# Routing tokens to sorted rows batch by batch, with each expert's weights fetched once

## The chip, the cores and the metric

The kernel runs on one core of a Trainium2 chip. The metric is device time in microseconds (us). A core has a matrix engine (TensorE, PE in the profile; its weight loads are PEld), a vector engine (VectorE, DVE), a scalar engine (ScalarE, ACT), a general one (GpSimd, POOL), a queue engine that issues transfers (SyncE, SP), and 16 DMA engines. SBUF is the memory on the chip, with 128 partitions; PSUM takes the results of TensorE in eight banks.

## The reference

Two blocks follow each other. The first is a gated linear recurrence over 768 steps for 4 batches and 8 heads of width 48; the second routes each of the 3072 tokens to one of 8 experts and scales the expert's output by the token's gate.

```python
# attention: batch 4, heads 8, seq 768, head_dim 48
scale = np.minimum(mag, 0.999) / (mag + 1e-06)      # mag = |a_re + i a_im|
for t in range(S):
    S_re, S_im = ar*S_re - ai*S_im + k_t (x) v_t, ar*S_im + ai*S_re
    y[:, :, t] = q_t . S_re
x = y.transpose(0, 2, 1, 3).reshape(3072, 384)
# experts: E = 8, D = 384, F = 1024
logits = x @ w_gate
expert_idx = np.argmax(logits, axis=1)
gate_w = softmax(logits)[arange, expert_idx]
for e in range(E):
    xe = x[expert_idx == e]
    out[expert_idx == e] = gate_w[..., None] * (np.maximum(xe @ w1[e], 0.0) @ w2[e])
```

With this input the experts get 354, 406, 392, 388, 370, 421, 338 and 403 tokens. Everything is float32.

## The kernel before

Attention is written as a list of operations with estimated durations, which a small list scheduler puts in order for each engine. Per batch: gates are loaded and limited, VectorE scans them (`front`), corrects (`fix`) and folds them into q and k (`fold`), packs go by DMA to head tiles (KX, QX), and TensorE does the chunked attention. At the end of a chunk of 128 tokens (last group of heads), the rows are transposed, multiplied with the gate's weights, and stored:

```python
if g == G - 1:
    rows = state["row", b, c]
    px = pe(6, across, rows, ...)            # 3 transposes of xf
    turned_x = act(DM, lambda: A.copy(xt, px_ps), [px], ...)
    lg = pe(3, logits, [turned_x], ...)      # lg_ps[:, c, :] = x @ wgate
    away = dma(5.0, lambda ...: Q.dma_start(x_hbm[r0:r0 + 128, 0:DM]..., xf[:, c, :]), rows)
...
copy = act(C * E, lambda: A.copy(lg_all[:, b * C:(b + 1) * C, :], lg_ps), [lg], first=1)
```

After attention comes a general path for gates that the fast scan cannot take: two loops whose count of trips, 0 here, is loaded into a register of every engine.

```python
n_blk = nc.values_load(trips[0:1, 0:1], min_val=0, max_val=S // BL, ...)
n_til = nc.values_load(trips[0:1, 1:2], min_val=0, max_val=NT, ...)
with tc.For_i(0, n_blk, 1) as i0:
    ...   # [cut: the recurrence step by step]
with tc.For_i(0, n_til, 1) as ti:
    ...   # [cut: logits of its rows]
```

Then all tokens are routed at once. Each expert's tokens fill whole tiles of 128 places, 31 tiles in all (`NTILE = NT + E - 1`), and two index tables are made: `idx`, the token at each place, and `widx`, the weight rows of each tile.

```python
tt(sub, lg_all, bc(red(lg_all, "mx", ALU.max)[:, :, None], full), ALU.subtract)
...   # [cut: softmax, one-hot, ranks by two matmuls, prefix sums, slots]
for t in range(NT):
    nc.tensor.matmul(ids, lhsT=A[:, t, :], rhs=V[:, t]..., start=(t == 0), stop=(t == NT - 1))
```

The expert part runs tile by tile. It gathers the rows and that tile's weights (3.1 MB) with indirect transfers:

```python
for j in range(NTILE):
    gather(xs, x_hbm[:, :], idx[:, j:j + 1])
    gather(w1t, w1[:, :], widx[:, j:j + 1])
    gather(w2t, w2[:, :], widx[:, j:j + 1])
    for d in range(DT):                                   # 3 transposes
        nc.tensor.transpose(xt_ps[:, d, :], xs[:, d * 128:d * 128 + 128], ident)
    nc.vector.tensor_copy(xt, xt_ps)
    for f in range(FT):                                   # 8 x 3 products, 128 columns
        for d in range(DT):
            nc.tensor.matmul(h_ps[:, f, :], lhsT=w1t[:, c:c + 128], rhs=xt[:, d, :], ...)
    nc.scalar.activation(ht[:, 0:FT // 2, :], h_ps[:, 0:FT // 2, :], func=ACT.Relu)
    nc.vector.tensor_scalar_max(ht[:, FT // 2:, :], h_ps[:, FT // 2:, :], 0.0)
    for f in range(FT):                                   # 8 products, 384 columns
        nc.tensor.matmul(o_ps, lhsT=ht[:, f, :], rhs=w2t[:, f * DM:f * DM + DM], ...)
    nc.vector.tensor_scalar_mul(y, o_ps, xs[:, DM:W])     # gate
    nc.gpsimd.indirect_dma_start(out=out[:, :], out_offset=...idx[:, j:j + 1]..., in_=y, ...)
```

Of the kernel before, what the change touches and what calls it, by code (L numbers as in the profile page):

```python
# [9 lines left out]
FP32 = mybir.dt.float32  # L10
# [23 lines left out]
W = DM + 1  # L34
LEAST = 1e-20
# [100 lines left out]
def gateloop_then_moe(ctx, tc, q, k, a_re, a_im, v, wg, w1, w2, out):  # L136
    nc = tc.nc
    x_hbm = nc.dram_tensor("x_hbm", (N + 1, W), FP32, kind="Internal").ap()

# [20 lines left out]
    with tc.tile_pool(name="zero", bufs=1) as setup:  # L160
        zrow = setup.tile([1, W], FP32, name="zrow")
        nc.vector.memset(zrow, 0.0)
        nc.sync.dma_start(x_hbm[N:N + 1, :], zrow)

# [30 lines left out]
    lg_all = route.tile([128, NT, E], FP32, name="lg_all")  # L195
    good = route.tile([128, B, G * C + 4], FP32, name="good")

    with ExitStack() as att:
# [14 lines left out]

        KXs = [buf(f"KX{i}", KW) for i in range(RING)]
# [8 lines left out]
        gates = [buf(f"gate{i}", JQ, 3, NC) for i in range(BL // JQ)]  # L223
        X = buf("X", BL, 2, NC)
        last, carry, zc = buf("last", 3, NC), buf("carry", 2, G * C, NB), [buf(f"zc{i}", 2, 2, G * C) for i in range(2)]
        lim = [[buf(f"{n}{i}", JQ, NC) for n in ("ls", "ll", "lu")] for i in range(2)]
        lsq, fsq = buf("lsq", JQ, 2, NC), buf("fsq", BL, 2, C * NB)
        fx = [buf(f"fx{i}", BL * C * (NB - 1)) for i in range(4)]
        zs = [buf(f"z{i}", 2, 2, NC) for i in range(2)]
# [4 lines left out]
        xf = buf("xf", C, DM)  # L234
# [6 lines left out]
        lg_ps = ps[7][:, 0:C * E].rearrange("p (c e) -> p c e", e=E)  # L241
# [16 lines left out]
        def dma(late, emit, after=(), free=()):  # L258
            return op("S", 0.62, late, emit, after, free)

# [161 lines left out]
        def attention(b, g):  # L422
# [24 lines left out]
            for c in range(C):  # L447
# [71 lines left out]
                if g == G - 1:  # L519
# [14 lines left out]
                    r0 = b * S + c * 128  # L534
                    away = dma(5.0, lambda c=c, r0=r0: Q.dma_start(x_hbm[r0:r0 + 128, 0:DM].rearrange("(n j) w -> j n w", j=BL), xf[:, c, :]), rows)
                    state["xf", c] = [away, px]
            for i in slots:
                state["head", i] = [y]
            if g == G - 1:
                copy = act(C * E, lambda: A.copy(lg_all[:, b * C:(b + 1) * C, :], lg_ps), [lg], first=1)  # L540
                state["lg"] = [copy]

        load_gates(0)
        limit(0)
        for b in range(B):
            front(b, range(G))
            fixed = [fix(t) for t in range(G)]
            for t in range(G):
                fold(b, t, fixed[t])
                attention(b, t)  # L550
            if b + 1 < B:
                load_gates(b + 1)
                limit(b + 1)
# [4 lines left out]
    with ExitStack() as fs:  # L558
        fp = fs.enter_context(tc.tile_pool(name="fp", bufs=1))
        fps = fs.enter_context(tc.tile_pool(name="fps", bufs=1, space=PSUM))  # L560
        nc.vector.tensor_scalar(out=good[:, :, G * C:], in0=good[:, :, G * C:], scalar1=MOST, scalar2=None, op0=ALU.is_le)
        least = fp.tile([128, 1], FP32, name="least")
        nc.vector.tensor_reduce(least, good.rearrange("p n c -> p (n c)"), axis=AX, op=ALU.min)
        ones_f = fp.tile([128, 1], FP32, name="ones_f")
        nc.vector.memset(ones_f, 1.0)
        n_good = fps.tile([1, 1], FP32, name="n_good")
        nc.tensor.matmul(n_good, lhsT=least, rhs=ones_f, start=True, stop=True)
        trips = fp.tile([1, 2], I32, name="trips")
        for u, n in enumerate((S // BL, NT)):
            nc.vector.tensor_scalar(out=trips[:, u:u + 1], in0=n_good, scalar1=127.5, scalar2=float(n),  # L570
                                    op0=ALU.is_lt, op1=ALU.mult)
        BG = B * G
        state = fp.tile([128, 2, BG, D], FP32, name="state")
        nc.gpsimd.memset(state, 0.0)  # L574

        own_i = fp.tile([128, G, H], I32, name="own_i")
        nc.gpsimd.iota(own_i, pattern=[[128, G], [-D, H]], base=0, channel_multiplier=1)
        own_f = fp.tile([128, G, H], FP32, name="own_f")
        nc.vector.tensor_copy(own_f, own_i)
        own = fp.tile([128, G, H], FP32, name="own")  # L580
        nc.vector.tensor_scalar(out=own, in0=own_f, scalar1=0.0, scalar2=None, op0=ALU.is_ge)
        nc.vector.tensor_scalar(out=own_f, in0=own_f, scalar1=float(D), scalar2=None, op0=ALU.is_lt)
        tt(own, own, own_f, ALU.mult)
        why = "0 or the whole count"
        n_blk = nc.values_load(trips[0:1, 0:1], min_val=0, max_val=S // BL, skip_runtime_bounds_check_because=why)
        n_til = nc.values_load(trips[0:1, 1:2], min_val=0, max_val=NT, skip_runtime_bounds_check_because=why)
        x_tok = x_hbm[0:N, 0:DM].rearrange("(b s) (h e) -> s h b e", b=B, e=D)
        with tc.For_i(0, n_blk, 1) as i0:
            a = fp.tile([128, 2, BG, BL], FP32, name="fa")
            qk = fp.tile([128, 2, BG, BL], FP32, name="fqk")  # L590
            for b in range(B):
                for t in range(G):
                    for o, src in ((a[:, 0], a_re), (a[:, 1], a_im)):
                        nc.sync.dma_start(o[:, b * G + t, :], src[b].rearrange("p j (t m) -> t m p j", t=G)[t, ds(i0, 1)])
                    for u, src in enumerate((q, k)):
                        nc.sync.dma_start(qk[:, u, b * G + t, :], src[b, :, t].rearrange("p j m -> m p j")[ds(i0, 1)])
# [260 lines left out]
```

## Time and profile before

| | |
|---|---|
| time, median of 3 runs | 772.2 us (771.48 to 775.8) |
| span of the profiled run | 766.3 us |
| TensorE busy | 602.1 us, 79% |
| VectorE busy | 387.1 us, 51% |
| ScalarE busy | 280.3 us, 37% |
| GpSimd busy | 137.8 us, 18% |
| moved by DMA | 156.5 MB, 108.4 MB of it by GpSimd's queue |

The profile gives busy time per engine over the span, the same in slices, and groups of instructions by line of the kernel, engine, and the tiles they write and read (`out<-in`). A line in order of time has a start, a length, the engine, the line, the operation, its tiles and shapes, a count, and in brackets how long the engine had been idle and what ended that. In attention all instructions carry the line of one helper (L132), so tile names tell them apart. A float32 product stands as two matrix instructions (1488 of `h_ps` are 31 x 24 x 2).

### The profile page before, as it was taken

The numbers are of one execution on the slowest core, as the hardware profiler recorded it, in microseconds if no ns is written. First come the engines' busy times: TensorE is split into PE (matmuls) and PEld (weight loads), VectorE is DVE, ScalarE is ACT, GpSimd is POOL, SyncE is SP. The second block draws the span as 40 slices with busy tenths as digits, with TensorE's granted clock in tenths as the row PEclk, the third lists the DMA queues.
The fourth block names the chain that finished last, engine by engine and source line by source line (L and its number), as shares of the span: only waits on it lengthen the run. The fifth ranks groups of instructions, "written<-read, shape, count | busy, mean of one in ns | idle before, by whom it ended". The sixth has DMA issues, their size and how long they took to land. (4 is left out here: it accounts for less than half of the span.)

```text
span 766.3 us, 11061 instructions
## 1 busy us (share of the span) xinstructions
PE 602.1 (79%) x3985; PEld 521.7 (68%) x3985; DVE 387.1 (51%) x720; ACT 280.3 (37%) x870; POOL 137.8 (18%) x160
## 2 busy tenths in 40 slices
PE   0000499789973999899317999999999999999997
PEld 0000499789963998899306787787787777787775
DVE  3999999989999999741261111111111111111111
ACT  4653799579985866775200000000000000000000
POOL 8000000000000000000112332342332442343221
PEclk9999999779985999999757999999999999999999
DMA  7131883486528706721019779789778988778930
GB/s 223 40 88 25 200 211 102 109 208 172 147 70 192 182 25 167 194 73 43 25 27 413 291 287 349 279 331 383 267 308 332 360 322 338 294 290 338 338 127 1
DMA packets 67630, 156.50 MB, mean 204 GB/s; under 512 B 9873, under 2 KB 50866, under 8 KB 59634
## 3 DMA queue, kind: packets, MB, share of 16 engines
q0 software_dynamic: 12896, 108.36, 36.9%
q1 hardware_dynamic: 51474, 47.36, 23.9%
q8 instruction: 33, 0.54, 0.3%
q10 hardware_dynamic: 3200, 0.01, 0.2%
q14 instruction: 27, 0.22, 0.1%
HBM read 127.23 MB, written 10.83 MB: 180 GB/s over the span
## 5 line engine op out<-in xcount | busy, mean ns | idle before, releaser
L804 PEld LDWEIGHTS h_ps<-xt,w1t 128*128 128x128 f32 x1488 | 172.9, 194 | 13.0 <-issue 5.0
L804 PE MATMUL h_ps<-xt,w1t 128*128 128x128 f32 x1488 | 173.2, 277 | 4.7 <-issue 4.7
L810 PE MATMUL o_ps<-w2t,ht 128*128 128x384 f32 x496 | 167.8, 492 | 8.5 <-ACT ht L806 8.2
L132 PE MATMUL bank<-QX,KX 128*128 128x224 f32 (+1 forms) x384 | 87.4, 367 | 102.6 <-DVE fl L132 86.1
L806 ACT ACTIVATE ht<-h_ps 128x512 f32<-128x512 f32 x31 | 18.5, 597 | 356.3 <-PE h_ps L804 356.3
L132 PEld LDWEIGHTS bank<-QX,KX 128*128 128x128 f32 x384 | 70.4, 207 | 105.0 <-issue 86.0
L810 PEld LDWEIGHTS o_ps<-w2t,ht 128*128 128x128 f32 x496 | 91.7, 190 | 71.7 <-ACT ht L806 14.2
L132 PE MATMUL bank<-st,QX 128*128 128x128 f32 x576 | 109.9, 279 | 1.7 <-ACT st L132 1.7
L812 DVE TENSOR_SCALAR yo<-o_ps,xs 128x384 f32<-128x384 f32 x31 | 19.2, 618 | 143.4 <-PE o_ps L810 143.4
L132 PEld LDWEIGHTS bank<-st,QX 128*128 128x128 f32 x576 | 87.9, 195 | 2.9 <-ACT st L132 2.9
L799 DVE COPY xt<-xt_ps 128x384 f32<-128x384 f32 x31 | 17.2, 556 | 139.4 <-PE xt_ps L797 139.4
L132 ACT ACTIVATE QX<-diag,KX 96x48 f32<-96x48 f32 x320 | 80.6, 329 | 3.8 <-DMA KX<-pk 3.7
L132 PE MATMUL bank<-vb,am 128*128 128x128 f32 x384 | 73.5, 282 | 4.9 <-DVE am L132 3.0
L813 POOL DMA_INDIRECT out_dram<-yo,idx x31 | 31.5, 1016 | 194.0 <-DVE yo L812 193.1
L132 PEld LDWEIGHTS bank<-vb,am 128*128 128x128 f32 x384 | 60.3, 196 | 6.6 <-DVE am L132 3.7
L574 POOL MEMSET state<- 128x1152 f32 x1 | 1.1, 1062 | 353.6 <-DMA x_hbm<-xf 353.6
L132 DVE TENSOR_TENSOR am<-bank,causal 128x256 f32<-128x256 f32 x120 | 43.0, 363 | 33.8 <-PE bank L132 28.9
L132 PE MATMUL bank<-vb,kt 128*128 128x128 f32 x320 | 59.4, 278 | 0.2 <-ACT kt L132 0.2
L132 PEld LDWEIGHTS bank<-vb,kt 128*128 128x128 f32 x320 | 48.2, 195 | 0.3 <-issue 0.3
L132 DVE TENSOR_TENSOR z<-gate,X 128x576 f32<-128x576 f32 x56 | 42.0, 750 | 0.6
L132 DVE TENSOR_TENSOR fx<-X,carry 128x672 f32<-128x672 f32 x48 | 38.5, 848 | 0.0
L785 POOL DMA_INDIRECT xs<-x_hbm,idx x31 | 30.2, 975 | 26.0 <-DVE idx L765 16.9
(143 smaller groups left out, 658.5 us busy)
## 6 DMA issues: line engine op xcount, KB each, us to landing
KX<-pk SPq DMA_DIRECT2D x48, 146.2 KB, 4.1
QX<-pk SPq DMA_DIRECT2D x48, 144.0 KB, 3.7
gate<-in_a_re_dram SPq DMA_DIRECT2D x16, 288.0 KB, 3.1
gate<-in_a_im_dram SPq DMA_DIRECT2D x16, 288.0 KB, 3.5
qt<-in_q_dram SPq DMA_DIRECT2D x12, 384.0 KB, 4.7
kt_in<-in_k_dram SPq DMA_DIRECT2D x12, 384.0 KB, 5.6
vb<-in_v_dram SPq DMA_DIRECT2D x24, 192.0 KB, 3.6
x_hbm<-xf SPq DMA_DIRECT2D x24, 192.0 KB, 2.9
```

Of the source, the lines that this page charges most:

```text
L132: return lambda *a, **kw: self.tc.keep_in_program_order(f(*a, **kw))
L574: nc.gpsimd.memset(state, 0.0)
L785: nc.gpsimd.indirect_dma_start(out=o, out_offset=None, in_=src, in_offset=bass.IndirectOffsetOnAxis(ap=index, axis=0))
L799: nc.vector.tensor_copy(xt, xt_ps)
L804: nc.tensor.matmul(h_ps[:, f, :], lhsT=w1t[:, c:c + 128], rhs=xt[:, d, :], start=(d == 0), stop=(d == DT - 1))
L806: nc.scalar.activation(ht[:, 0:FT // 2, :], h_ps[:, 0:FT // 2, :], func=ACT.Relu)
L810: nc.tensor.matmul(o_ps, lhsT=ht[:, f, :], rhs=w2t[:, f * DM:f * DM + DM], start=(f == 0), stop=(f == FT - 1))
L812: nc.vector.tensor_scalar_mul(y, o_ps, xs[:, DM:W])
L813: nc.gpsimd.indirect_dma_start(out=out[:, :], out_offset=bass.IndirectOffsetOnAxis(ap=idx[:, j:j + 1], axis=0), in_=y, in_offset=None, bou ...
```

## The change

The change moves the routing into attention and lays the tokens out by expert in memory, so that the expert part works expert by expert.

- A new tensor `sorted_x` has 3072 places for each expert; the first 448 (`CAP`) of each are blanked at the start (a token number past the end, so that the output's scatter drops the row).
- When a batch's logits are there (the last batch in two parts, of 4 and 2 chunks), `send` finds expert, gate and rank of its tokens, keeps the next free place of each expert (`free_row`), and scatters the rows, with gate and token number, from SBUF to `sorted_x`.
- Each expert's weights are fetched once with plain transfers; three buffers. The gates' buffers now stand first in SBUF, where the first weights go.
- An expert's 448 rows are one moving operand of 448 columns for the first product. The second has three tiles of 128 rows and a half tile of 64, whose two halves of 192 output columns go to the two halves of the array's columns.
- The general path (recurrence, routing and the old expert part) stands at the end as one loop of 0 or 1 trips; it also runs if an expert has over 448 tokens. Its count is loaded after the seventh expert.

It is there to take the routing off the way between the blocks, to load fewer weights and compute fewer padded rows.

```diff
+    sends = [(b, 0, C) for b in range(B - 1)] + [(B - 1, 0, 4), (B - 1, 4, C)]
...  # attention
-                    away = dma(5.0, lambda ...: Q.dma_start(x_hbm[r0:r0 + 128, 0:DM]..., xf[:, c, :]), rows)
+                    for n_send, (sb, c0, c1) in enumerate(sends):
+                        if (sb, c1 - 1) == (b, c):
+                            send(n_send, b, c0, c1 - c0, lg)
+        def send(k, b, c0, n, lg):
+            number = act(n, lambda: A.copy(xf[:, cs, DM + 1], token[...]), ...)
+            o = dve(wide, lambda: V.tensor_reduce(top, logit, axis=AX, op=ALU.max), [lg], free)
+            d = dve(wide, lambda: vtt(sub, logit, bc(top[:, :, None], full), ALU.subtract), [o])
+            x = act(wide, lambda: A.activation(ex, sub, func=ACT.Exp), [d], free)
+            o = dve(wide, lambda: vstt(pos, sub, 0.0, bc(rev[:, None, :], full), ALU.is_equal, ALU.mult), [d], free)
+            o = dve(wide, lambda: V.tensor_reduce(top, pos, axis=AX, op=ALU.max), [o])
+            one_hot = dve(wide, lambda: vtt(oh, pos, bc(top[:, :, None], full), ALU.is_equal), [o], free)
+            ...   # [cut: gate = 1 / sum of exps, three more on VectorE]
+            r = pe(n * 0.6, ranks, [one_hot], state.get("rank", []), first=0)      # n bf16 products
+            t = pe(n * 0.4, counts, [one_hot], state.get("count", []), first=0)    # n bf16 products
+            ...   # [cut: slot = sum((rank + free_row) * one_hot); free_row += count: four on VectorE]
+            for i in range(n):
+                move = pool_dma(4.0, lambda i=i: nc.gpsimd.indirect_dma_start(
+                    out=sorted_x[:, :], out_offset=...slot[:, i:i + 1]..., in_=xf[:, c0 + i, :], ...),
+                    [s, gate, number, state["blank"]] + state["row", b, c0 + i])
+        def blank():
+            for e in range(E):
+                nc.gpsimd.dma_start(sorted_x[e * N:e * N + CAP]..., bc(xf[0:64, 0:1, :], ...))
...  # between: general path and routing go to the end
...  # experts
+        psH = ms.enter_context(tc.tile_pool(name="psH", bufs=4, space=PSUM))
+        weights = [fetch(0), fetch(1)]
+        xs = load(0)
+        xt = turned(xs)                       # 3 x 4 transposes into 3 banks of 448 columns
+        for e in range(E):
+            xs_next = load(e + 1); weights.append(fetch(e + 2))
+            for f in range(FT):
+                h = psH.tile([128, CAP], FP32, name="h_ps")
+                for d in range(DT):
+                    T.matmul(h, lhsT=w1t[:, d, f * 128:f * 128 + 128], rhs=xt[:, d, :], ...)
+                ...   # [cut: relu into ht, ScalarE and VectorE in turn]
+            xt = turned(xs_next)
+            for i in range(TT):               # TT = 3
+                for f in range(FT):
+                    T.matmul(o, lhsT=ht[:, f, i * 128:i * 128 + 128], rhs=w2t[:, f, :], ...)
+                ...   # [cut: times the gate; scatter to out]
+            for f in range(FT):
+                for u in range(2):
+                    T.matmul(o[u * 64:u * 64 + 64, 0:HALF], lhsT=ht[:, f, TT * 128:CAP],
+                             rhs=w2t[:, f, u * HALF:u * HALF + HALF], ...)
+            ...   # [cut: times the gate; scatter to halves of out's rows]
+            if e == E - 2:
+                n_gen = nc.values_load(trips[0:1, 0:1], min_val=0, max_val=1, ...)
+    with tc.For_i(0, n_gen, 1):               # the general path, whole
```

(`[...]` and `...` in code stand for cuts; conditions on the last expert are left out.)

## The prediction

> **What bounds the kernel now.** I read the page's slices first, then a table of busy times by stage, then the order of time around each stage's border and inside one tile of the expert part.
>
> From the page, the slices (tenths busy in 40 slices of 19.2 us each):
>
> ```profile
> PE   0000499789973999899317999999999999999997
> DVE  3999999989999999741261111111111111111111
> PEclk9999999779985999999757999999999999999999
> ```
>
> Three stages show: VectorE full to about slice 16, TensorE full from slice 22 to the end, and a hollow of two slices between, in which TensorE's clock drops too. The stage table puts numbers on them (first column the stretch, then its length, then busy us and instructions of each engine, granted clock, DMA share, GB/s):
>
> ```profile
> 72.00:260.00 188.00, 147.08 (x1052) 142.75 (x1053) 184.58 (x320) 147.05 (x494) 0.00 (x0) 0.89 0.61 156
> 260.00:371.30 111.30, 106.68 (x831) 103.85 (x829) 71.47 (x141) 73.97 (x283) 0.00 (x0) 0.98 0.41 104
> 371.30:406.70 35.40, 2.94 (x31) 2.19 (x32) 16.82 (x63) 1.84 (x3) 9.02 (x15) 0.53 0.24 70
> 406.70:761.70 355.00, 345.42 (x2074) 272.93 (x2074) 54.03 (x92) 18.51 (x31) 112.42 (x116) 0.99 0.78 300
> ```
>
> Attention until 260 us: VectorE 184.58 of 188 us, so it sets the pace. From 260 to 371.3: TensorE 106.68 of 111.3. From 371.3 to 406.7 no engine is half busy: a chain of dependent steps. From 406.7: TensorE 345.42 of 355. DMA is 78% busy there, but TensorE does not wait for it. The hollow, in order of time (start, length):
>
> ```profile
> 370.45 0.83 PE L132 MATMUL bank<-wgate,xt 128*128 128x8 f32 x6 [0.57 <-ACT xt L132]
> ...
> 373.55 0.21 DVE L570 TENSOR_SCALAR trips<-n_good 1x1 int32<-1x1 f32 x2 [0.33 <-PE n_good L567]
> ...
> 379.89 0.35 DVE L683 TENSOR_REDUCE mx<-lg_all 128x24 f32<-128x192 f32 x1 [5.27 <-SPq L637]
> ...
> 397.28 0.19 DVE L765 SCALAR_TENSOR_TENSOR idx<-raw,emp 128x31 int32<-128x31 f32 x1
> 397.76 1.13 POOL L785 DMA_INDIRECT xs<-x_hbm,idx  x1 [16.91 <-DVE idx L765]
> ```
>
> The last logits end at 371.3; two loops of zero trips cost until 379.9; routing of all tokens lasts until 397.5; then come the gathers. And one tile of the expert part:
>
> ```profile
> 546.38 5.52 PE L804 MATMUL h_ps<-xt,w1t 128*128 128x128 f32 x48
> ...
> 551.74 0.49 PE L797 MATMUL xt_ps<-ident,xs 128*128 128x128 f32 x3
> 551.94 0.60 ACT L806 ACTIVATE ht<-h_ps 128x512 f32<-128x512 f32 x1 [10.88 <-PE h_ps L804]
> ...
> 552.59 4.81 PEld L810 LDWEIGHTS o_ps<-w2t,ht 128*128 128x128 f32 x16 [0.60 <-ACT ht L806]
> 552.59 5.43 PE L810 MATMUL o_ps<-w2t,ht 128*128 128x384 f32 x16 [0.36 <-ACT ht L806]
> ```
>
> h starts at 546.38 and the next tile's h at 557.86, so a tile costs 11.48 us; 31 tiles give 355.9. Each fp32 product is two records. Rates are start to start: (5.52 - 0.275)/47 = 0.1116 us for 128 columns, (5.43 - 0.492)/15 = 0.329 us for 384. The slope is 0.00085 us a column, so on the same line 448 columns cost 0.3835 and 192 cost 0.166. Attention's 224-column records (six in 1.30 us, 0.19 apart) lie on it.
>
> **What the Trainium skill says.** (1) FP8 and Floating Point Precision, TensorE Precision Notes: true FP32 takes four passes. The trace agrees: 2 x 0.1116 us for four passes of 128 columns. So only columns streamed count, and fewer, longer products save little per column. (2) TensorE: Matmul & The Clock Gate, Part 1: an idle array falls to half clock and needs about 3.4 us of work to recover. The trace agrees: 0.53 in the hollow, and the first tile's 48 products take 7.54 us in place of 5.52. (3) TensorEngine Tiling (Array Packing), Key Properties: column tiles of 64 work independently, and a change of tiling mode drains the engine. No row of this trace shows either; this is my weakest number. (4) DMA: Bandwidth & Descriptors, Anatomy of one DMA: about 2 us of each transfer is fixed, mostly the write receipt. Here a scatter to the output lands 2.9 us after issue (median of 31).
>
> **The change, part by part.** I computed the routing from the reference: experts get 338 to 421 tokens, so all fit in 448 and the general path runs zero times.
>
> *Expert part.* It computed 31 x 128 = 3968 rows and will compute 8 x 448 = 3584. Per expert: h, 24 products = 48 records of 448 columns, 48 x 0.3835 = 18.4 us; three full output tiles, 48 x 0.329 = 15.8; transposes, nine of 128 rows at 0.111 and three of 64 at about 0.08 = 1.2; a wait for the two transpose banks, 0.4. The half tile is 32 records of 192 columns: 32 x 0.166 = 5.3 if the two halves of the array take turns, 2.7 if they always overlap. I choose 3.8: overlap is plausible since the halves alternate, but each product is two dependent records on one half, and the mode is entered and left. Sum 39.6; times 8, less the last expert's missing transposes, 315.6. To that 2 us of cold clock as before, and 2 us because every engine, TensorE too, loads the loop's register after expert 6: 319.6. Against 355.0 this takes off 35.4. The 0.5 us that each tile waited between h and its outputs goes too; the transposes of the next expert now fill it. Weights fall from 31 x 3.1 MB to 8 x 3.1 MB; that saves no time, as TensorE did not wait for them.
>
> *The hollow.* Removed: the two loops (373.8 to 379.9), the routing of all tokens at once (to 397.5), the wait for the gathered weights (w1t issued at 399.2, h at 406.7). Weights 0 and 1 go into the space of the gates, free when the last batch's scan is over, and their loads stand in the queue right behind the last packs (issued at 334 to 337), so 6.3 MB at about 300 GB/s land before attention ends. In the hollow stay, for the last two chunks: five dependent VectorE steps at 0.2 to 0.25 and their order with the exp, 1.5; rank products 0.5; three steps 0.8; two scatters, 0.25 + 1.25 + 2.9 = 4.4; the load of expert 0 (0.8 MB in rows of 1.5 KB; 0.38 MB loads took 4.7 to 5.6), 5.0; twelve transposes at half clock and two copies, 3.3. Sum 15.5; with 1.5 for waits between queues, 17. Saved 35.4 - 17 = 18.4.
>
> *Attention.* Each send adds 12 small VectorE instructions at about 0.2 = 2.4 us. Those of batches 0 and 1 fall where VectorE is full: +4.8. That of batch 2 falls after 310 us, where VectorE is half idle. TensorE gets 24 small products in its own full stretch, about 0.08 each: +2. The stores of rows to memory leave the sync queue, and GpSimd, idle in attention, takes the scatters. The blanking of 5.5 MB stands at 12 to 60 us, where the DMA share is about 0.2; batch 0 sends first near 130, so it is hidden. At the start the new constants add about 1 us and the wait for the zero row (1.3) goes: nothing. Attention ends 7 later.
>
> *The end.* The last scatter as before; then the skipped loop. Two of them with their register loads took 6 us, so one costs 3: +3.
>
> Sum: -35.4 - 18.4 + 7 + 3 = -43.8, so 772.2 - 43.8 = 728.4; I say 728.
>
> **Rivals.** (A) *Half tiles take turns*: 5.3 in place of 3.8, and mode changes on top: +12 to +16, near 742. For it: each half's product still streams 192 columns of fp32. Against: the second half's weights need only their own columns. (B) *A queue of DMA waits replaces the routing*: if the scatters to the sorted rows wait for each other's landing (all write one tensor at unknown places), or the weight loads are not early, the hollow stays near 25: +8. For it: five transfers in sequence, each 3 to 5 us. Against: before, gathers were issued 1.25 us apart without waiting. (C) *Attention pays more*: TensorE works in order, and a rank product placed too early stalls it while VectorE, the bound, computes the one-hot. At 2 us a send this is +10; with A it gives 750. (D) *All goes well*: halves overlap and batches 0 and 1 hide their sends: -9 - 5, near 714.
>
> **Range and chances.** The expert part's 35 us rests on measured rates and on the arithmetic; A alone moves it by a third. The hollow's 18 could be 10 to 22. A and B together give 750, still under 757, the border of 2%. I take 712 to 748. Faster by over 2%: 0.94; within 2%: 0.05; slower: 0.01 (a stall that returns with every expert or send).
>
> **What would show it.** Right: h records about 0.383 apart and 18.4 us an expert; half tiles 3 to 5 us an expert; TensorE nearly full from about 395 to 715; logits ending at 375 to 381; h of expert 0 about 17 us after them; the first weights landed before; no wait of TensorE for DMA after that. Wrong: halves one after another (A), scatters spaced by their landing (B), TensorE waiting for the one-hot in attention (C), or TensorE waiting at each expert's start for rows or weights, which I price at zero.

## The result and the profile after

The changed kernel takes 804.7 us (median of 4, 803.9 to 805.6) against 772.1: ratio **1.041**, 95% interval 1.038 to 1.045. It was to be 728, so the prediction has the sign wrong. The profiled span went from 766.3 to 802.1 us. These are the slices of the changed kernel (20.05 us each):

```profile
PE   0000099946499868988796049999999999999991
DVE  4839999999479976994212001010101111111000
PEclk9999999977689869987998559999999999999996
DMA  7962575276341962085300490333241515010000
```

The expert part at the right is as full as it was to be, and it starts later: slices 22 and 23, the hollow, have hardly moved in width but stand some 60 us to the right of where they were. The loss lies ahead of them. VectorE, which sets the pace in attention's first half, was full from slice 1 to slice 15; now there is a hole in slice 2 (the digit 3) and another around slice 10 (4, 7). The table by stage (stretch, length, busy us and instructions of PE, PEld, DVE, ACT and POOL, clock, DMA share, GB/s), of the changed kernel:

```profile
40.00:60.00 20.00, 0.00 (x0) 0.00 (x0) 7.33 (x13) 5.71 (x8) 0.00 (x0) 1.00 0.61 144
...
373.00:434.00 61.00, 55.36 (x422) 53.69 (x422) 15.03 (x41) 31.73 (x129) 4.86 (x5) 0.94 0.15 42
434.00:475.30 41.30, 3.62 (x17) 2.20 (x16) 3.12 (x20) 0.75 (x2) 4.86 (x5) 0.50 0.62 226
475.30:785.80 310.50, 308.71 (x1111) 173.22 (x1110) 38.50 (x77) 30.39 (x55) 30.12 (x31) 0.99 0.25 90
785.80:802.10 16.30, 0.10 (x2) 0.00 (x0) 0.42 (x1) 0.00 (x0) 0.97 (x1) 0.61 0.04 15
```

With the borders that the prediction used (last logits, first h, last product, end):

| stage | before, us | foretold change | measured change |
|---|---|---|---|
| attention, to the last logits | 371.3 | +7 | **+62.7** (ends at 434.0) |
| hollow, to the first h | 35.4 | -18.4 | **+5.9** (41.3) |
| expert part | 355.0 | -35.4 | **-44.5** (310.5) |
| end | 4.6 | +3 | **+11.7** (16.3) |
| sum | 766.3 | -43.8 | +35.8 |

**The start.** In order of time, on the changed kernel, GpSimd's blanking, and VectorE's next work on gates:

```profile
19.40 5.83 POOL L633 DMA_DIRECT2D sorted_x<-xf  x8 [0.32 <-POOL xf L259]
...
52.53 0.76 DVE L134 SCALAR_TENSOR_TENSOR ls<-lsq 128x576 f32<-128x576 f32 x1 [15.97 <-ACT lsq L134]
```

The chain of waits (start, length, what) passes from the gates' transfer to it:

```profile
26.89 24.36 DMA gate<-in_a_im_dram
51.33 1.17 ACT lsq L134
```

A gate load, median 3.5 us in the kernel before, landed 24.4 us after its issue, with the blanks ahead of it, and VectorE stood idle for 16. From the list of the kernel before's transfers (KB each, median us from issue to landing):

```profile
gate<-in_a_im_dram SPq DMA_DIRECT2D x16, 288.0 KB, 3.5
```

These gates are the second batch's; but VectorE takes its work in the order of a list made beforehand, and that list expected them.

**The hollow.** From the last logits (434.0) on, in order of time:

```profile
438.12 0.97 POOL L620 DMA_INDIRECT sorted_x<-xf,slot  x1 [2.43 <-DMA sorted_x<-xf,slot]
441.57 0.97 POOL L620 DMA_INDIRECT sorted_x<-xf,slot  x1 [2.48 <-DMA sorted_x<-xf,slot]
...
448.67 0.97 POOL L620 DMA_INDIRECT sorted_x<-xf,slot  x1 [2.50 <-DMA sorted_x<-xf,slot]
452.01 0.33 SPq L663 DMA_DIRECT2D w<-in_moe_w_dram  x1
...
454.18 0.53 SPq L670 DMA_DIRECT2D xs<-sorted_x  x1
...
471.94 3.42 PE L134 MATMUL xt_ps<-ident,xs 128*128 128x128 f32 x12 [36.59 <-DMA xs<-sorted_x]
...
475.30 1.11 PE L134 MATMUL h_ps<-xt,w 128*128 128x448 f32 x1
```

Two things are to be seen. The scatters stand 3.4 to 3.6 us apart and each waits for the landing of the one ahead. And the first weights are asked for at 452.01, when the last scatter has landed, with the rows of expert 0 behind 6.3 MB of them: those rows arrive at 471.8.

**Attention.** Its waits (who waited for whom: total, times, longest), from 108 to 475 us:

```profile
ACT xf L134 <- DMA sorted_x<-xf,slot: 39.6, 17, 6.6
...
PE bank L134 <- ACT xf L134: 25.7, 11, 5.7
```

`xf` is the one buffer of rows. The next batch's rows can't be written into it before the scatter has read them, ScalarE waits in order, and TensorE waits for ScalarE: the spacing of the scatters (3.4 to 7.8 us within a batch) comes back as a stall of attention. In the kernel before the same wait of TensorE was small (60 to 372 us):

```profile
PE bank L132 <- ACT xf L132: 1.8, 3, 1.1
```

**One expert**, TensorE only, in order of time:

```profile
670.59 18.31 PE L134 MATMUL h_ps<-xt,w 128*128 128x448 f32 x48
688.73 2.23 PE L134 MATMUL xt_ps<-ident,xs 128*128 128x128 f32 x12
690.89 18.50 PE L134 MATMUL o_ps<-w,ht 128*128 128x384 f32 x80
709.32 5.15 PE L134 MATMUL h_ps<-xt,w 128*128 128x448 f32 x13
```

From h to h 38.73 us, without a gap; 18.14 for h, 2.16 for the transposes, 18.43 for the outputs. Taking the prediction's 15.8 for the three full tiles leaves 2.6 for the half tile's 32 records.

**The end**, in order of time:

```profile
784.09 0.97 POOL L689 DMA_INDIRECT out_dram<-yo,to  x1 [4.20 <-ACT yo L736]
785.95 0.42 DVE L744 TENSOR_SCALAR yh<-o_ps,xs 128x192 f32<-128x192 f32 x1 [7.30 <-PE o_ps L134]
787.89 0.97 POOL L689 DMA_INDIRECT out_dram<-yh,to  x1 [2.83 <-DVEq L756]
```

The last rows are ready at 786.4, go at 787.9, and the program ends 14.2 us after that.

### The profile page after: what moved, and what is told of

It is laid out like the page before. It is cut to its first block, busy times and chain, and to the rows that moved or that the text cites. A ratio compares the mean times of both kernels' runs of the same rounds, so it can differ in the third digit from the quotient of the medians.

```text
span 802.1 us, 9036 instructions
## 1 busy us (share of the span) xinstructions
PE 584.7 (73%) x3050; PEld 432.5 (54%) x3050; DVE 366.1 (46%) x714; ACT 294.5 (37%) x899; POOL 80.6 (10%) x101
## 4 chain that ended last, share of the span: by engine, by line
DMA 32%; issue 31%; PE 15%; DVE 14%; ACT 5%; SPq 1%; POOLq 0%; POOL 0%; DVEq 0%; ACTq 0%
PE bank L134 15%; DMA sorted_x<-xf,slot 10%; DMA out_dram<-yo,to 8%; DMA out_dram<-yh,to 4%; DMA gate<-in_a_im_dram 4%; DMA KX<-pk 3%; DVE fx L134 3%; DMA xs<-sorted_x 2%; DVE ls L134 2%; DVE X L134 2%; DVE z L134 2%; ACT QX L134 1%; DVE fs L134 1%; DVE am L134 1%; DMA qt<-in_q_dram 1%
## 5 line engine op out<-in xcount | busy, mean ns | idle before, releaser
L134 PE MATMUL h_ps<-xt,w 128*128 128x448 f32 x384 | 148.1, 546 | 1.1 <-issue 1.1
L134 PE MATMUL o_ps<-w,ht 128*128 128x384 f32 (+1 forms) x640 | 147.9, 424 | 0.0
L134 PEld LDWEIGHTS o_ps<-w,ht 128*128 128x128 f32 (+1 forms) x640 | 90.1, 169 | 56.0 <-issue 4.7
L134 PEld LDWEIGHTS h_ps<-xt,w 128*128 128x128 f32 x384 | 73.1, 192 | 72.3 <-issue 72.2
L134 PE MATMUL bank<-vb,am 128*128 128x128 f32 x384 | 78.4, 297 | 26.5 <-ACT xf L134 25.7
L134 DVE TENSOR_TENSOR am<-bank,causal 128x256 f32<-128x256 f32 (+1 forms) x120 | 42.8, 366 | 69.0 <-PE bank L134 67.8
L723 DVE TENSOR_SCALAR ht<-h_ps 128x448 f32<-128x448 f32 x32 | 20.0, 624 | 105.2 <-PE h_ps L134 105.2
L620 POOL DMA_INDIRECT sorted_x<-xf,slot x24 | 27.0, 1127 | 397.4 <-DVE z L134 169.2
L689 POOL DMA_INDIRECT out_dram<-yo,to x24 | 23.3, 972 | 288.1 <-ACT yo L736 254.6
L134 PE MATMUL xt_ps<-ident,xs 128*128 128x128 f32 x96 | 18.3, 299 | 37.2 <-DMA xs<-sorted_x 36.6
L134 ACT ACTIVATE xf<-bank 128x48 f32<-128x48 f32 (+2 forms) x120 | 22.8, 236 | 52.8 <-DMA sorted_x<-xf,slot 33.0
## 6 DMA issues: line engine op xcount, KB each, us to landing
sorted_x<-xf POOLq DMA_DIRECT2D x8, 675.5 KB, 15.8
```

The source lines that it names most:

```text
L134: return lambda *a, **kw: self.tc.keep_in_program_order(f(*a, **kw))
L620: move = pool_dma(4.0, lambda i=i: nc.gpsimd.indirect_dma_start(out=sorted_x[:, :], out_offset=bass.IndirectOffsetOnAxis(ap=slot[:, i:i + ...
L689: nc.gpsimd.indirect_dma_start(out=rows, out_offset=bass.IndirectOffsetOnAxis(ap=index, axis=0), in_=y, in_offset=None, bounds_check=rows. ...
L723: nc.vector.tensor_scalar_max(ht[:, f, :], h, 0.0)
```

## The experiments

The theory after this reading: three causes, each in a stretch of its own. (1) The blanks, 5.5 MB in one lump, delay whatever is loaded beside them. (2) The scatters wait for each other. (3) The weights are asked for too late. The rivals: that one of them is only another seen from its far end, or that the sends' own instructions cost more than the 7 us that I gave them. All ratios are to the kernel before, run on the same chip; the changed kernel's is 1.0412.

### Blanks later in the list (late_blank)

```diff
-        state["blank"] = pool_dma(50.0, blank, sum((state["raw", i] for i in range(BL // JQ)), []))
+            if b == 0:                       # one list entry for each expert, behind the scan
+                state["blank"] = [pool_dma(6.0, lambda e=e: blank(e), after[e]) for e in range(E)]
```

> Only the blanking moves: the transfers for experts 0 to 3 wait for the end of batch 0's scan, those for 4 to 7 for its corrections, in place of all eight starting at 19.4 us. Theory (the blanking's 5.5 MB held back batch 1's gate loads, and ScalarE's queue stood behind one of them from 33 to 51 us): VectorE has no idle stretch before 60 us, all later marks come 15 to 18 us earlier, time 786 to 790. Rival (the loads of gates would be late anyway, or the blanking only moves its harm to the packs at 72 us and after): time 798 to 806.

Measured: 805.7 us, ratio 1.047 (1.045 to 1.049). The timeline says why nothing is learnt of the blanks from it:

```profile
19.40 5.85 POOL L632 DMA_DIRECT2D sorted_x<-xf  x8 [0.32 <-POOL xf L259]
```

They still went at 19.40. A place in a list doesn't hold back a transfer whose data is there and whose queue is empty; it takes data that isn't there yet. The later runs use that.

### Scatters that don't wait for each other (no_order)

Their rows never overlap, so the order between them is declared away; nothing else changes.

```diff
+        def apart(move):                     # move: a row scatter
+            for old in sent_rows:
+                tc.declare_no_dep(move.ins, old.ins, reason="other rows")
+            sent_rows.append(move)
-                move = pool_dma(4.0, lambda i=i: nc.gpsimd.indirect_dma_start(out=sorted_x[:, :], ...),
+                move = pool_dma(4.0, lambda i=i: apart(nc.gpsimd.indirect_dma_start(out=sorted_x[:, :], ...)),
```

> Only the order among the 24 row scatters is dropped, which write different rows: each still waits for its own data and for the blanking. Theory (each scatter waits for the landing of the one before, 3.4 us apart, and the next batch's rows wait for the buffer they leave): scatters 1.25 us apart, no long wait of ScalarE's xf for a scatter, attention shorter by 35 to 45 us, the hollow before the experts shorter by 12 to 15, time 745 to 760. Rival (attention is longer because of the sends' own 12 VectorE instructions and TensorE's in-order wait for the one-hot): attention shorter by under 10 us, time 780 to 792.

Measured: 762.2 us, ratio **0.992** (0.991 to 0.994). In order of time:

```profile
195.86 1.39 POOL L627 DMA_INDIRECT sorted_x<-xf,slot  x1 [0.30 <-ACT kt L134]
197.55 1.36 POOL L627 DMA_INDIRECT sorted_x<-xf,slot  x1 [0.30 <-issue]
...
402.64 0.97 POOL L627 DMA_INDIRECT sorted_x<-xf,slot  x1 [0.30 <-issue]
406.02 0.33 SPq L670 DMA_DIRECT2D w<-in_moe_w_dram  x1
...
425.98 3.42 PE L134 MATMUL xt_ps<-ident,xs 128*128 128x128 f32 x12 [25.99 <-DMA xs<-sorted_x]
```

The scatters now stand 1.3 to 2.7 us apart. The last logits end at 398.7 in place of 434.0 (35.3 us), the hollow is 30.7 in place of 41.3; I had expected 35 to 45 us in attention, 12 to 15 in the hollow and at most 760 us. The waits that were 39.6 and 25.7 us are, over the same stretch,

```profile
PE bank L134 <- ACT xf L134: 7.1, 4, 3.3
...
ACT xf L134 <- DMA sorted_x<-xf,slot: 5.6, 3, 2.3
```

By the ratios this one wait is worth (1.0412 - 0.9924) x 772.1 = 37.7 us. It is the largest cause, and most of it lay in attention, not in the hollow.

### Buffers that wait for what lies in their own place (tile_waits)

In the changed kernel the first weights waited for the last scatter, though it doesn't read the memory that they go to: a new pool of buffers waits for all that the old pool in its memory held. Here each buffer waits for what lies under it alone.

```diff
-        wp = ms.enter_context(tc.tile_pool(name="wp", bufs=3))
+        wp = ms.enter_context(tc.tile_pool(name="wp", bufs=3, reuse_waits="tile"))
         # the same for mp, psX, psH and psO
```

> Only the pools of the expert part change how they reuse memory: each tile waits for the tiles it lies on, not for everything of the attention's pool. Theory (the first weights were asked for only at 452 us because the pool waited for the last scatter): weights 0 and 1 are asked for before attention ends and have landed by the last scatter; expert 0 then waits for its rows alone, 5 us of load and 3.4 of transposes; the hollow is 14 to 18 us shorter, time 787 to 791. Rival (6.3 MB beside the last packs and scatters slow these, or the queue's order holds the weights back anyway): time 797 to 806.

Measured: 794.9 us, ratio 1.033 (1.030 to 1.035); a gain, and smaller than expected (787 to 791 us): the hollow is 30.0 us, 11.3 shorter and not 14 to 18. In order of time, the second buffer's request and the scatter beside it:

```profile
433.33 0.33 SPq L663 DMA_DIRECT2D w<-in_moe_w_dram  x1
...
443.45 0.97 POOL L620 DMA_INDIRECT sorted_x<-xf,slot  x1 [7.45 <-DMA sorted_x<-xf,slot]
```

Weights 0 came early (397), weights 1 only now, in the middle of the scatters, one of which then took 8.4 us in place of 3.5.

### No general path (no_general)

The loop of zero trips and the load of its count are left out; attention, experts and output stay.

> The general path at the end is left out, with the loading of its count after expert 6 (so there is no answer for inputs that the fast path can't take). Theory (skipping the loop costs about 9 us after the last landing at 791.8, and the load of the count about 1 to 2): the end comes 3 to 4 us after the last scatter's issue, time 793 to 796. Rival (the end is drain and the landing of the last scatters, whatever follows): time 802 to 805.

Measured: 797.1 us, ratio 1.037 (1.035 to 1.039), not clear of the changed kernel's interval. The medians alone differ by 7.6 us, where I had expected 793 to 796 us and under 4 us from the last scatter to the end. The profile shows where. The last half tile's weight loads and the last scatter, in order of time, with the span ending at 795.5:

```profile
784.05 2.47 PEld L134 LDWEIGHTS o_ps<-w,ht 128*64 128x64 f32 x32 [0.55 <-issue]
...
788.40 0.97 POOL L689 DMA_INDIRECT out_dram<-yh,to  x1 [2.37 <-DMA out_dram<-yo,to]
```

7.1 us from there to the end, against 14.2 with the loop: skipping it costs **7.1 us** there. Another 0.5 us lies ahead of it: with the loop the last scatter was released by VectorE's queue at the loop (L756), without it by the landing of the scatter ahead. TensorE's 1.15 us ahead of the last expert, for the count, is gone as well. The 32 weight loads of the half tile pass in 2.47 us, which fits the 2.6 of the reading above.

### Blanks behind the first scan, by data (late_blank2, order_blank)

VectorE writes the source row of the blanks behind the scan; so they can't go earlier. Once on the changed kernel, once on no_order.

```diff
+        def zero_row():
+            V.memset(xf[0:64, C - 1, 0:DM + 1], 0.0)
+            V.memset(xf[0:64, C - 1, DM + 1:WS], 4.0 * N)
+                row0 = dve(DM, zero_row, state["carried", 0], first=0)
+                state["blank"] = [pool_dma(6.0, lambda e=e: blank(e), [row0]) for e in range(E)]
```

> The changed kernel, with the eight blanking transfers held back until VectorE has written their source row behind the first batch's scan, so that the batch's gate values are loaded first (this time by data and not by a place in a list). Theory (blanking of 5.5 MB at the start delays the gates and with them VectorE, the bound of attention's first half): 15 to 17 us less than the changed kernel, ratio to the kernel before near 1.020. Rival (VectorE's late start is due to its own new constants, or the time comes back at the waits of the row stores): 0 to 3 us less, ratio 1.037 to 1.041.

> The same late blanking on top of the version whose 24 row scatters don't wait for each other (ratio 0.992). Theory (the two costs are separate and add up): again 15 to 17 us less, ratio 0.971. If the wait for each other's landing had only been the late start seen from its other end, less than 5 us: ratio over 0.985. If attention then still ends more than 15 us after the kernel before's, the sends' own instructions cost more than the 7 us that I predicted.

Measured: 811.6 us, ratio 1.057 (1.055 to 1.059), and 772.9 us, 1.006 (1.004 to 1.008): both **slower** than what they started from, by 12 and 10 us. I had expected 15 to 17 less. The stage table of order_blank, and its sync queue in order of time:

```profile
20.00:60.00 40.00, 0.00 (x0) 0.00 (x0) 39.38 (x68) 23.23 (x38) 0.00 (x0) 1.00 0.21 60
...
100.00:140.00 40.00, 23.95 (x146) 22.36 (x146) 18.81 (x39) 20.06 (x78) 0.00 (x0) 0.74 0.97 216
```

```profile
92.20 18.52 SPq L134 DMA_DIRECT2D KX<-pk  x8
```

The kernel before, for comparison:

```profile
20.00:60.00 40.00, 0.00 (x0) 0.00 (x0) 39.38 (x70) 23.42 (x39) 0.00 (x0) 1.00 0.21 60
...
100.00:140.00 40.00, 39.67 (x312) 39.07 (x311) 39.79 (x86) 36.50 (x127) 0.00 (x0) 1.00 0.55 147
```

From 20 to 60 VectorE is full again: the start is mended. But the list put the blanks at 91 to 97 us, just when the heads' rows, q and k are moved, and there VectorE loses 21 of 40 us; eight requests of the sync queue took 18.5 us in place of 5.5. A part of this loss has another way: the blanks' source is a row of `xf`, and ScalarE waited 7.0 us for them before it could write there. So the theory as I had put it (late is good) fell, and what it rests on (bytes in one lump hold back others) was seen twice.

### Blanks one at a time (paced), and fewer of them (tail_blank)

Both on no_order. The first spreads the eight transfers over the scan; a VectorE write of the row's last column sets each free. The second leaves them in their old place and leaves out the blanks of each expert's first 320 places, which these inputs fill.

```diff
 # paced: inside the scan of batch 0, after steps 2, 3, 5, 7, 8, 10, 12 and 14
+                        V.memset(source(e)[:, 0, DM + 1:WS], 4.0 * N)      # a source row of its own for each e
+                    state["blank"].append(pool_dma(6.0, lambda e=e: blank(e), [m]))
```

```diff
 # tail_blank
-                nc.gpsimd.dma_start(sorted_x[e * N:e * N + CAP]..., bc(xf[0:64, 0:1, :], [64, CAP // 64, WS]))
+                nc.gpsimd.dma_start(sorted_x[e * N + 320:e * N + CAP]..., bc(xf[0:64, 0:1, :], [64, (CAP - 320) // 64, WS]))
```

> The version whose row scatters don't wait for each other (ratio 0.992), with the eight blanking transfers spread over the first batch's scan, one at a time between about 24 and 60 us, where the DMA engines were 21 to 27% busy in the kernel before. Theory (5.5 MB take some 30 us of all DMA engines; asked for in one lump they delay whatever is loaded then, the gates at 20 us, rows of heads and q and k at 95 us; where nobody waits they cost nothing): attention ends 14 to 17 us earlier than without pacing, ratio 0.971 to 0.975, and 30 us earlier than with the lump at 91 us. Rival (the memory traffic costs VectorE the same wherever it stands, or attention's growth sits in the sends): under 6 us less, ratio over 0.985.

> The version whose row scatters don't wait for each other, with the blanking at its old place but only for places 320 to 447 of each expert (1.6 MB in place of 5.5; that leaves out the blanks of the first 320 places, which these inputs overwrite in any case). Theory (it is the bytes of the lump at 20 us that hold back the gates): the transfers take about 8 us and the gates land in time, so again 14 to 17 us less, ratio 0.970 to 0.975, without anything moved. Rival (it is the queue's start, or the order of the list, that starts VectorE late): 0 to 5 us less.

Measured: 749.5 us, ratio **0.971** (0.964 to 0.977), and 747.2 us, ratio **0.969** (0.964 to 0.974). The stage table of paced:

```profile
20.00:60.00 40.00, 0.00 (x0) 0.00 (x0) 38.66 (x73) 22.52 (x38) 6.54 (x9) 1.00 0.76 198
...
100.00:140.00 40.00, 39.71 (x315) 39.52 (x313) 39.72 (x88) 37.28 (x132) 0.00 (x0) 1.00 0.49 133
```

and of tail_blank:

```profile
20.00:60.00 40.00, 0.00 (x0) 0.00 (x0) 39.38 (x70) 23.40 (x39) 4.32 (x8) 1.00 0.39 99
```

Same bytes, same 40 us, DMA three quarters busy, and VectorE full; or fewer bytes at the old place, and VectorE full. The rival (the list or the queue) falls. The lump cost (0.9924 - 0.9706) x 772.1 = 16.8 us, 12 to 22 by the two intervals.

The profiles show this at the first row scatter, which goes at 179.0 us in place of no_order's 194.5. By the last logits only 6.1 of these 15.5 us are left (392.6 against 398.7). In paced's execution the issue of batch 0's second scatter took long:

```profile
180.38 6.74 POOL L635 DMA_INDIRECT sorted_x<-xf,slot  x1 [0.30 <-ACT kt L134]
```

In no_order's execution it took 1.39 us, and batch 1's first scatter, the next mark, is ahead of no_order's by 9.6. The same 6.74 us stand in the profiles of tail_blank, order_blank, early_w and all_four, and 1.39 in paced_early's. So the last logits of two single executions can differ by some 6 us for this alone; what makes this scatter slow stays open.

### Weights early (early_w, on order_blank; paced_early, on paced)

Each of the three weight buffers is a pool of its own, so that the second waits no more for the heads' buffers.

```diff
-        wp = ms.enter_context(tc.tile_pool(name="wp", bufs=3))
+        wps = [ms.enter_context(tc.tile_pool(name=f"wp{i}", bufs=1, reuse_waits="tile")) for i in range(3)]
-            w = wp.tile([128, DT * F + FT * DM], FP32, name="w")
+            w = wps[e % 3].tile([128, DT * F + FT * DM], FP32, name="w")
         # mp, psX, psH, psO: reuse_waits="tile"
```

> The last version, and the expert part's buffers wait only for what lies in their own places (each of the three weight buffers a pool of its own). Theory (the first 6.3 MB of weights are asked for only when the last scatter has landed, and the rows of expert 0 queue behind them): weights asked for near 340 us, the rows of expert 0 landed some 6 us after the last scatter and h 3 us later, so the hollow falls from 31 to about 16 us: 13 to 15 us less than the last version, ratio near 0.953. Rival (the hollow is set by the chain of scatter landing, row load, transposes at a low clock, whatever the weights do): 0 to 4 us less.

> Paced blanking, row scatters that don't wait for each other, and weights asked for early, together. Theory (the three costs stand in different stretches and add): the hollow is 14.4 us instead of 30.7, so 15 to 16 us less than the paced version alone: ratio 0.951 to 0.956, some 735 us on the scale of 772. Rival (a later end of attention hid part of the weights' gain): ratio over 0.965.

Measured: early_w 752.2 us, ratio 0.979 (0.976 to 0.982), 20.5 us under order_blank where I expected 13 to 15 (16.1 in the hollow, 2.2 in attention, by the profiles); paced_early **731.1 us, ratio 0.952** (0.945 to 0.958), 14.7 under paced, near the 15 to 16 that I expected. In early_w, in order of time:

```profile
375.19 1.07 SPq L672 DMA_DIRECT2D w<-in_moe_w_dram  x1
...
415.88 0.98 POOL L625 DMA_INDIRECT sorted_x<-xf,slot  x1 [0.31 <-issue]
...
418.76 0.38 SPq L679 DMA_DIRECT2D xs<-sorted_x  x1
...
422.96 3.42 PE L134 MATMUL xt_ps<-ident,xs 128*128 128x128 f32 x12 [9.74 <-DMA xs<-sorted_x]
426.31 19.74 PE L134 MATMUL h_ps<-xt,w 128*128 128x448 f32 x48
```

The weights are in before the last logits (411.9), and the hollow is 14.4 us in place of order_blank's 30.5: 4.0 to the last scatter, 2.9 to its landing, 4.2 for the rows, 3.4 for the transposes. paced_early computes all that the reference asks for, general path included, and is the fastest complete version.

### Output scatters without order (all_four, on early_w)

```diff
+            for old in stored:               # the 32 scatters to out
+                tc.declare_no_dep(move.ins, old.ins, reason="other rows")
+            stored.append(move)
```

> The last version, and the 32 scatters to the output don't wait for each other either. Theory: only the last one counts, which waited about 1.5 us for the landing of the one ahead of it: 1 to 2 us less, ratio near 0.951. Rival (they hold back the expert part too, through the output buffers): over 5 us less.

Measured: 752.6 us, ratio 0.980 (0.979 to 0.982): no difference from early_w. The last scatter goes 2.6 us after the one ahead of it, no longer 3.5; the expected gain of 1 to 2 us, if there is one, is below what these runs tell apart.

### What is left in attention (no_scatter, no_send)

In paced_early the last logits end at 385.7, still 14.4 after the kernel before's. Both runs start from it and leave work out: no_scatter the 18 row scatters of batches 0 to 2, no_send the whole sends of these batches. The output rows of their tokens are missing, so these times are prices and not versions.

```diff
 # no_scatter
-            for i in range(n):
+            for i in range(n if b == B - 1 else 0):
                 move = pool_dma(4.0, ...)
 # no_send
                         if (sb, c1 - 1) == (b, c):
+                            if b < B - 1:            # the counts are copied on, nothing else
+                                continue
                             send(n_send, b, c0, c1 - c0, lg)
```

> The fastest version so far (paced blanks, scatters that don't wait for each other, early weights; ratio 0.952, last logits at 385.7 us, 14.4 after the kernel before's), with the 18 row scatters of batches 0 to 2 left out; their routing is still computed, and the output rows of those tokens are left out. Theory (what is left of attention's growth is TensorE waiting for row buffers that the scatters of the batch before still read): last logits 6 to 10 us earlier, near 378, ratio 0.939 to 0.944. Rival (it is the sends' arithmetic on VectorE, as I priced it, and the order of the list): under 3 us earlier, ratio over 0.947.

> The same with the whole sends of batches 0 to 2 left out: their 12 small VectorE steps, the rank and count products and the scatters (a copy of the counts stays; the output rows of those tokens are left out). Beside the run without scatters it gives the price of the arithmetic: 5 to 7 us by my prediction (4.8 on VectorE, 2 on TensorE), so ratio 0.932 to 0.938 and last logits at 372 to 374, near the 371.3 of the kernel before. If last logits stay over 378, something else in attention costs: the blanks even where they are paced, or the changed order.

Measured: ratio 0.932 (0.930 to 0.933) and 0.922 (0.920 to 0.923). The last logits of no_scatter, then of no_send:

```profile
380.41 0.84 PE L134 MATMUL bank<-wgate,xt 128*128 128x8 f32 x6 [0.57 <-ACT xt L134]
```

```profile
372.10 0.83 PE L134 MATMUL bank<-wgate,xt 128*128 128x8 f32 x6 [0.57 <-ACT xt L134]
```

The sends' arithmetic costs (0.9319 - 0.9215) x 772.1 = 8.0 us by the times and 8.3 by the last logits; I had said 7. Without sends attention ends at 372.9, 1.6 after the kernel before's, so what else the change does in attention adds up to almost nothing. The scatters themselves cost 4.4 us by the last logits (6 to 10 expected) and 15.2 by the ratios; the runs of paced_early lie at 727 and at 735, and the profile is of one at 727. I give 4 to 15 and not a number.

### A second buffer of rows (two_rows, ring5)

Batches take turns in two buffers of rows; the memory comes from the heads' ring, 5 places for 6. ring5 is the control, with the short ring alone.

```diff
-RING = 6
+RING = 5
-        xf = buf("xf", C, WS)
+        xfs = [buf("xfa", C, WS), buf("xfb", C, WS)]       # xf = xfs[b % 2] in attention and send; two_rows alone
```

> The fastest complete version (ratio 0.952), with a second buffer of rows, so that batch 1's rows don't wait for the scatters of batch 0; the memory for it is taken from the heads' ring, 5 places in place of 6. Theory (the scatters cost attention their hold on the row buffer, 10 to 15 us): nearly what leaving them out gave, less what the shorter ring costs: ratio 0.935 to 0.942, and 8 us or more under the shorter ring alone. Rival (the scatters' traffic or the placing of the list costs, not the buffer): as the shorter ring alone, within 4 us.

> The fastest complete version with 5 places in the heads' ring and one buffer of rows, the control for the last run. Theory: the sixth place gives the list a few us of freedom, so 2 to 8 us slower than with 6, ratio 0.955 to 0.962.

Measured: 738.7 us, ratio 0.962 (0.959 to 0.965), and 745.9 us, ratio 0.970 (0.967 to 0.974). two_rows lies 0.0085 x 772.1 = 6.6 us under ring5, between what the theory and the rival asked for; ring5 lies 14.4 over paced_early, nearly twice the most that I expected, so the exchange loses. Neither number is the price of a buffer alone, since the list comes out in another order each time. Among ring5's waits from 60 to 400 us stands

```profile
PE bank L134 <- DVE oh L134: 14.3, 2, 7.3
```

TensorE stood for products whose one-hot was not there yet, which is the prediction's rival C. The attention of paced_early and of two_rows has no such wait, and TensorE waited for the rows' two buffers 1.3 us in two_rows. So ring5's 14.4 us are as large as these waits, though that they are the whole cause is not shown, and neither is the gain of the second buffer by itself. How the scatters' 4 to 15 us divide between the row buffer, their traffic and the list's order stays open.

## Why the prediction was wrong

**The blanking, "so it is hidden": wrong, 16.8 us.** I took a mean DMA share of about 0.2 for 12 to 60 us (that holds from 20 us on, 0.21; over 12 to 60 it is 0.34) and the time by which the rows are needed (130). I did not ask who else loads in that stretch, and how late that may come. In the kernel before gates are loaded there too, in small amounts and on time, and VectorE's order counts on it. The Trainium skill, DMA: Bandwidth & Descriptors, Queues, rings and completion order, says that each DMA engine takes turns between the queues that have work for it; so a queue of its own gives blanks no lane of their own. The trace agrees so far: a gate load of another queue took 24.4 us in place of a median 3.5. That taking turns accounts for all of this is not shown. paced shows that the same bytes leave VectorE full where they are dosed (38.66 of 40 us).

**Attention +7: wrong, +62.7.** The term that I did price, the sends' instructions, measured 8 where I had 7, although TensorE gets 48 small products and not the 24 that I counted. What the sum lacked are the waits. By the last logits of the profiles: 434.0 in the changed kernel, 398.7 without the scatters' order (35.3), 385.7 with paced blanks and early weights (13.0), 381.3 without the first scatters (4.4), 372.9 without their sends (8.3), 371.3 in the kernel before. Each is one execution, and the slow scatter that some have moves the mark by some 6 us. Rival B named the right mechanism, scatters that wait for each other's landing, but priced it at +8 and in the hollow alone. I had argued against it with the gathers of the kernel before, issued 1.25 us apart: each of those wrote a tile of its own, while all 24 scatters write one tensor at places known only at run time. And I carried the wait only to the next scatter. Its way back, scatter to row buffer to ScalarE to TensorE, is what cost most. Rival C, TensorE waiting for the one-hot, plays no part in the changed kernel: the one such wait, 1.1 us, lies in the hollow. But it is real: with a ring of 5 the list places two such products so that TensorE waits 14.3 us.

**The hollow -18.4: wrong, +5.9.** The working of 17 us was sound: with scatters and weights as I had assumed them it measured 14.4 (early_w). Two assumptions failed. "Their loads stand in the queue right behind the last packs": the requests waited for the whole of the old pool, the last scatter included; 30.7 - 14.4 = 16.3 us. And the last six scatters stand in a row: 41.3 - 30.7 = 10.6 us.

**The expert part -35.4: right in kind, better in size, -44.5.** h took 18.14 us (18.4 foretold), the transposes 2.2 (1.6 with their wait), the outputs 18.4 (19.6). The half tile took 2.6 us where I had chosen 3.8 between 2.7 and 5.3: rival A, the halves in turn, falls. The change of tiling that the Trainium skill, TensorEngine Tiling (Array Packing), Key Properties, tells of shows no gap of its own here; its statement that tiles work independently is borne out, with 32 records of 192 columns at 0.08 us each, where the prediction's line through 128 and 384 columns (an estimate) gives 0.166 for one after another.

**The end +3: wrong in size, +11.7.** One skipped loop costs 7.1, not 3 (no_general), and another 0.5 ahead of the last scatter. Of the other 4.1, 0.7 is the last scatter's wait for the landing of the one ahead, and 3.4 lies behind its issue: without the loop 7.1 us pass from there to the end, where the kernel before needed 3.7. Why is open.

Together: the expert part gave more than I claimed, and three waits of which my sum had none took it back. With these three removed the ratio is 0.952, and 728 would have been 0.943.

## What to carry to other kernels

Before calling a transfer hidden, ask what else is loaded in the same stretch and who consumes it in a fixed order: dose it, or cut its bytes, and do not simply move it. When several writes go to one tensor at computed places, price them at landing to landing unless their independence is declared, and follow the wait back to the buffer that each write reads. A load is early only if what its buffer waits for is early; find that wait before counting on it.

## What the runs showed of the hardware that I had not expected

- The landing of a scatter went by what loaded beside it, not by its bytes. Each expert's scatter of 128 half rows (192 floats) goes just when the next weights and rows are asked for, and takes 5.5 to 6.4 us from issue to landing for the first five experts; for the sixth, with rows alone beside it, 3.75; for the seventh, with the DMA engines 2% busy, 2.6. That is the median of the scatters of 128 whole rows (384 floats), so half the bytes save nothing here. How many rows are kept doesn't explain the difference: the fifth and the seventh expert (370 and 338 tokens) keep none in this scatter.
- Scatters of 128 rows of 386 floats can be issued every 1.28 us; when each waits for the landing of the one before, every 3.45 in the hollow.
- A crowded set of DMA engines slows the issuing queue as well: eight requests of the sync queue took 18.5 us in place of 5.5.
- Two half tiles in the two column halves of the array overlap in fp32: 2.6 us for what would, by the prediction's estimate, be 5.3 in turn.
- Skipping a loop of zero trips at the end cost 7.1 us, two of them with their loads 6 in the middle of the kernel before.
